# The routing's values in between in a PSUM bank, and the high-half casts of the tokens' rows on ScalarE

## The chip, the cores and the metric

The kernel runs on one core of a Trainium2 chip. The metric is the time of one execution in device microseconds. The engines are called as the profile calls them: PE (TensorE), DVE (VectorE), ACT (ScalarE), POOL (GpSimd) and SP (SyncE, which here issues DMAs).

## What is computed

Linear attention with random features for 8 batches, 8 heads, 576 tokens and a head width of 64, followed by a mixture of experts in which each token goes to one expert:

```
phi(x)  = exp(h - max(h)) / sqrt(128),  h = x @ omega.T - |x|^2 / 2        # q, k scaled by 64^-1/4
attn    = phi(q) @ (phi(k).T @ v) / (phi(q) @ sum(phi(k)) + 1e-6)          # per batch and head
x       = attn, heads side by side                                         # 4608 tokens x 512
e       = argmax(x @ w_gate);  g = softmax(x @ w_gate)[e];  s = sigmoid(x @ w_output_gate)[e]
out     = g * s * (relu(x @ w1[e]) @ w2[e])                                # 8 experts, 512 -> 1024 -> 512
```

## The kernel before

The tokens are worked through in four superchunks (j = 0 to 3) of two batches each, nine blocks of 128 tokens. For each superchunk and head there is a unit (32 in all): PE projects keys and queries (line 503, tiles pp), DVE takes the extreme value of each row (line 525) and makes the bias nb (lines 534 and 538, or 531), ACT takes the exponentials (ef, line 544), PE sums keys times values (kv, line 637), ACT or DVE splits them (kvs), PE multiplies by the queries (pn, line 681), and DVE divides (den and xf, lines 690 to 694). Nearly all products are made of fp16 pairs: a high half by a cast, and the low half as the difference, which POOL computes (lines 437, 567, 588, 715).

Two units make a pair (16 in all). Its rows xf are split into a high half (step xh, line 711, a cast on DVE with one instruction for a unit) and a low half (step xl, line 715, POOL), both in the tile xs. From there one DMA writes the rows to DRAM and another transposes them (xrt); PE makes the logits of the gates (lg, line 777), and DVE adds them up (lga).

When the four pairs of a superchunk have their logits, its routing runs, nearly all of it on DVE, in short instructions on 8 to 144 numbers a partition. The steps are called route (which expert), gates, gate_exps (ACT) and weigh (the weight of each token), counts (PE), ranks and places (each token's place within its expert). Then a listing turns it into slots of 128 tokens of one expert: table, assign, lists, pid (PE), gi, controls, and advance, which prepares the state for the next listing (the last listing has limits in its place). Up to 8, 8, 9 and then 24 slots come of the four listings. For each slot POOL gathers its rows (gx, line 1344), a DMA transposes them, PE runs the two layers of the expert (lines 1381 and 1404), ACT and DVE make the halves between them (lines 1388 and 1392), and POOL scatters the result (line 1445). Weights that change are split by ACT (line 365) and DVE (line 369). The helper `small` gives each routing value a place in SBUF under its name (r_l, r_oh, r_sm and so on), one buffer each.

The order of the work is made by a planner when the program is built. Every step has an engine, an assumed cost, the steps it comes after, a rank, and, if it needs one, a PSUM bank, which it holds until a named step frees it. There are eight banks: five of class a, three of class b (for the experts), and class e, which takes any of the eight. The planner walks through an assumed time and always takes the step that can start first, by rank among near ties. Each engine then runs its steps in that order and waits at each for what it needs.

Of the kernel before, what the change touches and what calls it, by code (L numbers as in the profile page):

```python
# [12 lines left out]
I32 = mybir.dt.int32  # L13
# [82 lines left out]
C_END = C_CHUNK + NSC * NC  # L96


def constants():
    c = np.zeros((P, C_END), np.float32)  # L100
    e = np.arange(NE)
    c[:, C_RDESC:C_LT] = np.tile(NE - e, NC)
    turn = (FIRST - e) % NE
    c[:, C_LT:C_EIDX] = (turn[None, :] < turn[:, None]).reshape(-1)
    c[:, C_EIDX:C_ITEM] = e
    c[:, C_ITEM:C_PART] = np.arange(NITEM)
    c[:, C_PART] = np.arange(P)
    c[:, C_CHUNK:C_END] = np.arange(NSC * NC) * P
# [148 lines left out]
def attention_moe(ctx: ExitStack, tc: tile.TileContext, kqt, kqn, v, om, wg, w1, w2, cf, cm, ci, out):  # L257
# [31 lines left out]
    last = const.tile([P, 1], F32, name="last")  # L289
    nc.vector.memset(last, float(FIRST) if SPECULATE else -1.0)  # L290
# [38 lines left out]
    def first_state():  # L329
        nc.vector.tensor_scalar(cnt, eidx, float(KEY * P), None, ALU.mult)  # L330
        nc.vector.tensor_scalar(done[:, 0, :], eidx, float(KEY), None, ALU.mult)
        nc.vector.tensor_copy(done[:, 1, :], eidx)
        nc.vector.tensor_copy(ahead, cft[:, C_LT : C_LT + NE * NE].rearrange("p (a b) -> p a b", a=NE))
# [120 lines left out]
    def unit(u):  # L454
# [255 lines left out]
        def hi_half():  # L710
            nc.vector.tensor_copy(halves(xs(pr).bitcast(F16)[:, :, o : o + D]), halves(xf(pr)[:, :, o : o + D]))  # L711

        def lo_half():
# [6 lines left out]
            ("xh", u), ("DVE",), 0.37, hi_half, after=[("xf", u, 0), ("xf", u, 5)], rank=R + 6,  # L720
# [87 lines left out]

    rt = {}

    def route(j):
        l2 = lga(j).rearrange("p c (a e) -> p c e a", a=2)
        l = small("l", [NC, 2 * NE])
        nc.vector.tensor_reduce(out=l, in_=l2, op=ALU.add, axis=AX.X)
        yield
        lgt, log = l[:, :, 0:NE], l[:, :, NE:]
        top = small("top", [NC])
        nc.vector.tensor_reduce(out=top, in_=lgt, op=ALU.max, axis=AX.X)
        yield

        oh = small("oh", [NC, NE])
        nc.vector.tensor_tensor(out=oh, in0=lgt, in1=bc(top), op=ALU.is_ge)
# [9 lines left out]
        nc.vector.tensor_tensor(out=one, in0=oh, in1=bc(rm), op=ALU.is_equal)  # L832
        rt[j] = dict(one=one, lgt=lgt, log=log, top=top)

    def gates(j):
        r = rt[j]
        d = small("d", [NC, NE])
        nc.vector.tensor_tensor(out=d, in0=r["lgt"], in1=bc(r["top"]), op=ALU.subtract)
        yield
        z = small("z", [NC, NE])  # L840
# [3 lines left out]
        nc.vector.tensor_reduce(out=zs, in_=z, op=ALU.add, axis=AX.X)  # L844
        r.update(d=d, zs=zs)
# [6 lines left out]
    def weigh(j):  # L852
        d, zs = rt[j]["d"], rt[j]["zs"]
        sm = small("sm", [NC])
        nc.vector.tensor_reduce(out=sm, in_=d, op=ALU.add, axis=AX.X)
        yield
        nc.vector.tensor_scalar(sm, sm, 1e-9, 1.0 / S_OUT, ALU.add, ALU.mult)
# [25 lines left out]
    def ranks(j):  # L883

        pos = banks["pos", j]
        pk = small("pk", [NC, NE])
# [8 lines left out]
        rank = small("rank", [NC])  # L895
# [3 lines left out]
    def places(j):  # L899

        rank, key = rt[j]["rank"], keys[:, j * NC : (j + 1) * NC]
        ri = small("ri", [NC], I32)
# [20 lines left out]
    def table(g):  # L923

        t = tabs[g] = {}
        av_i = small("av_i", [NE], I32)
# [4 lines left out]
        av = t["av"] = small("av", [NE])  # L931
        nc.vector.tensor_tensor(out=av, in0=av_i, in1=done[:, 0, :], op=ALU.subtract)
        yield
        t8 = small("t8", [NE, NE])
# [5 lines left out]
        start = t["start"] = small("start", [NE])  # L940
# [3 lines left out]
        off = t["off"] = small("off", [2, NE])  # L944
        nc.vector.tensor_copy(off[:, 1, :], eidx)
        yield
        nc.vector.tensor_tensor(out=off[:, 0, :], in0=done[:, 0, :], in1=start, op=ALU.subtract)
        yield
        end = t["end"] = small("end", [NE])
        nc.vector.tensor_tensor(out=end, in0=start, in1=av, op=ALU.add)  # L950

    def assign(g):
# [9 lines left out]
        ends, mine = per_slot("ends", [], K, [NE]), per_slot("mine", [], K, [NE])  # L962
# [4 lines left out]
        ex = t["ex"] = small("ex", [2, max(KS) + 1])[:, :, 0 : K + 1]  # L967
# [4 lines left out]
        both = per_slot("both", [2], K, [NE])  # L972
# [9 lines left out]
        key = t["key"] = per_slot("key", [], K)  # L982
# [3 lines left out]
    def lists(g):  # L986
# [3 lines left out]
        if g == NG - 1:  # L990
            itc = ef(FREE).rearrange("p c m -> p (c m)").bitcast(F16)[:, 0 : nt * 2 * K]
            itc = itc.rearrange("p (c a i) -> p c a i", a=2, i=K)
        else:
            itc = small("itc", [NSC * NC, 2, max(EARLIER)], F16)[:, 0:nt, :, 0:K]
# [17 lines left out]
    def controls(g):  # L1012
# [5 lines left out]
        here = per_slot("here", [], K)  # L1018
# [3 lines left out]
        nc.vector.tensor_tensor(out=sw, in0=ex[:, 1:], in1=ex[:, 0:K], op=ALU.not_equal)  # L1022
# [33 lines left out]
    def advance(g):  # L1056
# [3 lines left out]
        t1 = small("t1", [NE])  # L1060
# [7 lines left out]
        fin = per_slot("fin", [], K)  # L1068
# [4 lines left out]
        nc.vector.tensor_tensor(out=fin, in0=fin, in1=t["ex"][:, 1, 1:], op=ALU.mult)  # L1073
# [3 lines left out]
        turn = small("turn", [NE])  # L1077
        nc.vector.tensor_scalar(turn, eidx, last, float(NE), ALU.is_gt, ALU.mult)
        yield
# [5 lines left out]
            in1=turn.unsqueeze(2).broadcast_to([P, NE, NE]),  # L1085
# [26 lines left out]
    def routing(j):  # L1112
# [10 lines left out]
        chain("route", (0.37, 0.14, 0.14, 0.14, 0.14, 0.14), route, first, tiles=[("lga", j)])  # L1123
# [9 lines left out]
        chain("gates", (0.14, 0.14, 0.14), gates, [("route", j)], rank=R + 5)  # L1133
        plan.add(("gate_exps", j), ("ACT",), 0.42, lambda: gate_exps(j), after=[("gates", j)], rank=R + 5)
        chain("weigh", (0.14, 0.07, 0.07, 0.08, 0.1), weigh, [("gate_exps", j)], rank=R + 5)
# [3 lines left out]
        )  # L1139

    def listing(g):
# [10 lines left out]
        chain("table", (0.07, 0.07, 0.08, 0.13, 0.08, 0.14, 0.08, 0.08, 0.08), table, [("ranks", j), *old])  # L1152
        chain("assign", (wide, wide, 0.07, wide, 2 * wide, 2 * wide, 0.08), assign, [("table", g)])
        each = 0.06 + 0.001 * nt * K
        own = [("ef", FREE)] if g == NG - 1 else []
        chain("lists", (each, each, each), lists, [("assign", g), ("places", j)], tiles=own)
# [6 lines left out]
        if g < NG - 1:  # L1163
            chain(
                "advance", (0.07, 0.07, 0.08, 0.08, 0.08, 0.08, 0.08, 0.08, 0.08, 0.13), advance, [("controls", g)],
                rank=R + 40,
            )
        else:
            chain("limits", (0.08, wide, wide, 0.08, 0.08, 0.08, 0.08), limits, [("assign", g)], rank=R + 0.5)
# [371 lines left out]
```

## Time and profile before

| | |
|---|---|
| Three runs | 701.48 us median (699.2 to 703.88) |
| Profiled execution | 700.21 us, its span on the core 698.4 us |
| Busy in the span | PE 613.5 us, DVE 444.4, ACT 406.1, POOL 326.6 |
| Mean granted clock of PE | 0.948 |

The span runs from the first to the last instruction. An engine's busy time counts what it executes, and includes time in which an instruction has started and can't go on. In rows of groups the numbers behind the bar are busy us, mean ns of one, and the idle time of the engine just before, with what ended it. In rows of the timeline the first two numbers are start and length in us, and the brackets hold the idle time before. In rows of windows the first number behind the stretch is its length, then come the engines' busy times.

### The profile page before, as it was taken

The page shows a single profiled execution, that of the slowest core. Times are in us where ns is not written, and L with a number is a line of the kernel's source. Part 1 is how long each engine was busy: PE and PEld are TensorE (multiplying, and loading weights), DVE is VectorE, ACT ScalarE, POOL GpSimd, SP SyncE. Part 2 cuts the span into 40 slices and gives each one's busy share as a digit, 9 for nine tenths or more (in the row PEclk, how much of TensorE's full clock was granted, in tenths as well). Part 3 has the DMA queues.
Part 4 walks back from the last instruction along what each step waited for, and adds up shares of the span by engine and source line. Part 5 has one row for each costly group of instructions (what it writes and reads, how often), then busy time and mean ns, then how long its engine had stood idle before and what let it go on. Part 6 is the DMA issues. An engine that isn't in the chain of part 4 may idle for free. (4 is left out here: it accounts for less than half of the span.)

```text
span 698.4 us, 22925 instructions
## 1 busy us (share of the span) xinstructions
PE 613.5 (88%) x8763; PEld 471.3 (67%) x8763; DVE 444.4 (64%) x1260; ACT 406.1 (58%) x909; POOL 326.6 (47%) x207
## 2 busy tenths in 40 slices
PE   6999974888897987599979869999999899999982
PEld 6899863856674765577747637887777576776750
DVE  4997898966577789688648788663583521341160
ACT  5967795878686773797858538772341421431150
POOL 1333253568673875689827637964122121231210
PEclk9999996899998999799989989999999999999997
DMA  8656889999999996999999976769956634832630
GB/s 276 235 141 165 260 257 222 176 267 225 294 304 274 177 250 113 213 208 296 212 299 232 222 134 159 148 121 190 313 127 176 211 84 109 291 75 70 246 116 8
DMA packets 181033, 137.78 MB, mean 197 GB/s; under 512 B 139535, under 2 KB 162575, under 8 KB 179600
## 3 DMA queue, kind: packets, MB, share of 16 engines
q1 hardware_dynamic: 174800, 116.13, 68.2%
q0 software_dynamic: 6080, 19.72, 9.2%
q8 instruction: 83, 1.36, 0.8%
q14 instruction: 70, 0.57, 0.3%
HBM read 83.69 MB, written 19.69 MB: 148 GB/s over the span
## 5 line engine op out<-in xcount | busy, mean ns | idle before, releaser
L1381 PE MATMUL ph<-xt,w1h 128*128 128x128 f16 (+1 forms) x2432 | 205.0, 218 | 1.5 <-DMA xt<-gx 1.4
L544 ACT ACTIVATE ef<-pp,nb 128x128 f32<-128x128 f32 x576 | 164.2, 392 | 70.0 <-DVE nb L538 34.5
L1381 PE MATMUL ph<-xt,w1l 128*128 128x128 f16 (+1 forms) x1216 | 201.3, 218 | 0.4 <-DVEq L1305 0.4
L1381 PEld LDWEIGHTS <-w1h 128*128 128x128 f16 x2432 | 182.0, 99 | 8.7 <-DMA xt<-gx 1.6
L1392 DVE SCALAR_TENSOR_TENSOR hl<-ph,hh 128x512 f16<-128x512 f32 (+1 forms) x76 | 50.5, 666 | 128.9 <-ACTq L1310 77.9
L567 POOL TENSOR_TENSOR es<-ef,es 128x1152 f16<-128x1152 f32 x44 | 104.7, 2384 | 43.6 <-ACT es L565 22.6
L1404 PE MATMUL po<-w2h,hl 128*128 128x512 f16 x304 | 119.6, 393 | 5.4 <-DVE hl L1392 5.4
L1404 PE MATMUL po<-w2h,hh 128*128 128x512 f16 x304 | 120.1, 395 | 4.5 <-DVE w1l L369 2.4
L1404 PE MATMUL po<-w2l,hh 128*128 128x512 f16 x304 | 119.6, 393 | 0.0
L1381 PEld LDWEIGHTS <-w1l 128*128 128x128 f16 x1216 | 118.8, 99 | 0.6 <-DVEq L1305 0.6
L525 DVE TENSOR_REDUCE pp<-pp 128x3 f32<-128x384 f32 x192 | 102.7, 558 | 22.1 <-PE pp L503 21.7
L1344 POOL DMA_INDIRECT gx<-rows,gi x38 | 40.5, 1067 | 162.9 <-ACT os L1456 119.8
L1404 PEld LDWEIGHTS <-hh 128*128 128x128 f16 x608 | 57.3, 100 | 70.0 <-issue 9.9
L1388 ACT ACTIVATE hh<-ph 128x512 f16<-128x512 f32 (+1 forms) x76 | 44.7, 589 | 75.0 <-PE ph L1381 66.4
L1456 ACT ACTIVATE os<-po,gx 128x512 f32<-128x512 f32 x38 | 26.1, 687 | 92.5 <-PE po L1404 80.3
L715 POOL TENSOR_TENSOR xs<-xf,xs 128x576 f16<-128x576 f32 x32 | 41.1, 1285 | 64.5 <-DVE xs L711 27.5
L437 POOL TENSOR_TENSOR xlo<-xt,xhi 128x1152 f16<-128x1152 f32 x24 | 57.2, 2381 | 20.0 <-ACT xhi L430 20.0
L1404 PEld LDWEIGHTS <-hl 128*128 128x128 f16 x304 | 30.8, 101 | 45.0 <-DVE hl L1392 6.4
L503 PE MATMUL pp<-omh,xhi 64*128 64x128 f16 x432 | 45.3, 225 | 17.4 <-ACT ef L544 5.5
L565 ACT CAST es<-ef 128x1152 f16<-128x1152 f32 x44 | 51.6, 1176 | 10.7 <-DMA et<-es 8.0
L503 PEld LDWEIGHTS <-xhi 64*128 64x128 f16 x864 | 35.0, 98 | 29.1 <-issue 9.4
L681 PE MATMUL pn<-kvs,et 128*128 128x65 f16 (+1 forms) x960 | 41.2, 199 | 10.2 <-DVE kvs L659 4.1
(159 smaller groups left out, 1015.0 us busy)
## 6 DMA issues: line engine op xcount, KB each, us to landing
r<-w SPq DMA_DIRECT2D x10, 2048.0 KB, 9.4
xt<-kqt SPq DMA_DIRECT2D x32, 576.0 KB, 5.5
xn<-kqn SPq DMA_DIRECT2D x24, 576.0 KB, 7.3
rawv<-v SPq DMA_DIRECT2D x32, 325.0 KB, 5.3
rows<-xs SPq DMA_DIRECT2D x16, 576.0 KB, 5.8
r<-w SPq DMA_DIRECT2D x8, 512.0 KB, 10.3
ef<-w SPq DMA_DIRECT2D x2, 512.0 KB
et<-w SPq DMA_DIRECT2D x2, 512.0 KB, 7.6
```

Of the source, the lines that this page charges most:

```text
L437: lambda t0=t0, t1=t1: nc.gpsimd.tensor_tensor(out=xl(u)[:, t0:t1], in0=xt32(u)[:, t0:t1], in1=xh(u)[:, t0:t1], op=ALU.subtract),
L503: nc.tensor.matmul(banks["pp", 2 * u + i, g][:, c, :], x[r, t], w[r, :], start=(a == 0), stop=(a == len(ops) - 1))
L525: nc.vector.tensor_reduce(out=pp[:, 3, 0:3], in_=pp[:, 0:3, :], op=ALU.min, axis=AX.X)
L544: nc.scalar.activation(ef(n)[:, c, :], banks["pp", n, g][:, c % 3, :], AF.Exp, bias=nb(n)[:, c : c + 1], scale=-SK)
L565: nc.scalar.copy(es(slot_es(n))[:, 0], ef(n))
L567: nc.gpsimd.tensor_tensor(out=es(slot_es(n))[:, 1], in0=ef(n), in1=es(slot_es(n))[:, 0], op=ALU.subtract)
L681: nc.tensor.matmul(pn[lo:hi, c - c0, :], a[:, c, lo:hi], w[:, b, :], start=(i == 0), stop=(i == len(ops) - 1))
L715: nc.gpsimd.tensor_tensor(out=x[:, :, P + o : P + o + D], in0=xf(pr)[:, :, o : o + D], in1=x[:, :, o : o + D], op=ALU.subtract)
L1381: nc.tensor.matmul(ph[:, f4, 0:w_], w[qd][:, kk, fo : fo + P], xt(n)[:, x, 0:w_], start=(a == 0), stop=(a == 3 * KC - 1))
L1388: nc.scalar.activation(hh(n)[:, sl, 0:w_], banks["ph", n, g][:, :, 0:w_], AF.Relu)
L1392: nc.vector.scalar_tensor_tensor(out=hl(n)[:, sl, 0:w_], in0=banks["ph", n, g][:, :, 0:w_], scalar=0.0, in1=hh(n)[:, sl, 0:w_], op0=ALU.ma ...
L1404: nc.tensor.matmul(po, x(n)[:, f, :], w[f // 2][:, f % 2, :], start=(f == 0 and a == 0), stop=(f == FC - 1 and a == 2))
```

## The change

The values that a routing and its listing need only for themselves move from SBUF into one PSUM bank of 512 numbers a partition, called rt. The bank is taken at the first step of route and freed at the end of advance (in the last listing, limits). A table gives each name its place in the bank; names that aren't alive together share one. Values stay in SBUF that ACT, PE or a DMA reads, that outlive the listing, that are fp16, or that meet a PSUM value as the second operand; for some of these a copy is made (avs, exs, turns). For the last listing most values of the slots stay in SBUF. Fifty-six DVE instructions of each of the first three routings and listings then read or write the bank, and 32 of the last.

Beside that, the expert numbers in off are written once at the start and not by each listing; the sum with 1 in weigh is joined with the product behind it; the first three listings build their list matrix from one comparison and one wider product with cp, a copy of constants in the bank; the ranks of gates and of advance put these steps earlier; table waits for gates, and advance for lists, weigh and places. The planner's assumed costs follow.

The casts xh run on ACT with an assumed cost of 0.6 in place of 0.37 on DVE.

```diff
-            nc.vector.tensor_copy(halves(xs(pr).bitcast(F16)[:, :, o : o + D]), halves(xf(pr)[:, :, o : o + D]))
+            nc.scalar.copy(halves(xs(pr).bitcast(F16)[:, :, o : o + D]), halves(xf(pr)[:, :, o : o + D]))
...
-            ("xh", u), ("DVE",), 0.37, hi_half, after=[("xf", u, 0), ("xf", u, 5)], rank=R + 6,
+            ("xh", u), ("ACT",), 0.6, hi_half, after=[("xf", u, 0), ("xf", u, 5)], rank=R + 6,
...
+    def inner(j, nm, sh, dt=F32):
+
+        a, n = HOMES[nm]
...
+        t = banks["rt", j][:, a : a + size]
...
-        l = small("l", [NC, 2 * NE])
+        l = inner(j, "l", [NC, 2 * NE])
...
-        oh = small("oh", [NC, NE])
+        oh = inner(j, "oh", [NC, NE])
...
-        sm = small("sm", [NC])
+        sm = inner(j, "sm", [NC])
...
-        nc.vector.tensor_scalar(zs, zs, 1.0, None, ALU.add)
-        yield
-        nc.vector.tensor_tensor(out=sm, in0=sm, in1=zs, op=ALU.mult)
+        nc.vector.scalar_tensor_tensor(out=sm, in0=zs, scalar=1.0, in1=sm, op0=ALU.add, op1=ALU.mult)
...
+        t["av"] = small("avs", [NE])
+        nc.vector.tensor_tensor(out=t["av"], in0=av_i, in1=done[:, 0, :], op=ALU.subtract)
...
-        start = t["start"] = small("start", [NE])
+        start = t["start"] = inner(j, "start", [NE])
...
-        off = t["off"] = small("off", [2, NE])
-        nc.vector.tensor_copy(off[:, 1, :], eidx)
...
+            cp = inner(GROUPS[g], "cp", [nt, 2])
+            nc.vector.tensor_copy(cp, cft[:, C_BOTH : C_BOTH + 2 * nt].rearrange("p (c a) -> p c a", a=2))
...
-        turn = small("turn", [NE])
+        turn = inner(GROUPS[g], "turn", [NE])
         nc.vector.tensor_scalar(turn, eidx, last, float(NE), ALU.is_gt, ALU.mult)
+        yield
+        turns = small("turns", [NE])
+        nc.vector.tensor_tensor(out=turns, in0=turn, in1=eidx, op=ALU.subtract)
...
-        chain("route", (0.37, 0.14, 0.14, 0.14, 0.14, 0.14), route, first, tiles=[("lga", j)])
+        chain(
+            "route", (0.37, 0.14, 0.14, 0.14, 0.14, 0.14), route, first, tiles=[("lga", j)],
+            bank=("e", ("rt", j), [512]),
+        )
...
-        chain("gates", (0.14, 0.14, 0.14), gates, [("route", j)], rank=R + 5)
+        chain("gates", (0.14, 0.14, 0.14), gates, [("route", j)], rank=R + 0.1)
...
-                rank=R + 40,
+                [("controls", g), ("lists", g), ("weigh", j), ("places", j)], rank=R + ADV, frees=[("rt", j)],
```

Every engine's order is planned anew, and differs in many places. Three of them follow. In the rows a name with a number is a tile and its buffer, and the line numbers are those of the kernel that the row is of.

DVE in the second routing, at the table of experts and the weights of the tokens, before (line 857 is the scaling of the sums r_sm):

```order
L938 TENSOR_REDUCE r_tot<-r_av 128x1
L857 TENSOR_SCALAR r_sm<-r_sm 128x9
L941 TENSOR_REDUCE r_start<-r_t_5322 128x8
L859 TENSOR_SCALAR r_zs<-r_zs 128x9
L945 COPY r_off<-cft 128x8
L861 TENSOR_TENSOR r_sm<-r_sm,r_zs 128x9
L947 TENSOR_TENSOR r_off<-done,r_start 128x8
L863 RECIPROCAL scales<-r_sm 128x9
L950 TENSOR_TENSOR r_end<-r_start,r_av 128x8
L657 TENSOR_SCALAR kvs_5441<-kv_5325 128x130
```

The same place on DVE now, where rt_5103 is the bank:

```order
L975 TENSOR_REDUCE r_tot<-rt_5103 128x1
L892 TENSOR_SCALAR rt_5103<-rt_5103 128x9
L978 TENSOR_REDUCE rt_5103<-rt_5103 128x8
L894 SCALAR_TENSOR_TENSOR rt_5103<-r_zs,rt_5103 128x9
L982 TENSOR_TENSOR off<-done,rt_5103 128x8
L896 RECIPROCAL scales<-rt_5103 128x9
L985 TENSOR_TENSOR rt_5103<-rt_5103,r_avs 128x8
L531 TENSOR_REDUCE pp_0_5203<-pp_0_5203 128x3
```

Two instructions are gone, the others stand in the same order with an operand in the bank, and a reduction of the attention follows in place of the split kvs, which moved ahead of this piece.

DVE at the end of the second advance, before:

```order
L1075 TENSOR_REDUCE last<-r_fin 128x1
L538 SCALAR_TENSOR_TENSOR nb_5749<-pp_0_5201,sqs_3982 128x3
L1078 TENSOR_SCALAR r_turn<-cft,last 128x8
L525 TENSOR_REDUCE pp_1_5232<-pp_1_5232 128x3
L1080 TENSOR_TENSOR r_turn<-r_turn,cft 128x8
L534 SCALAR_TENSOR_TENSOR pp_1_5232<-pp_1_5232,sqs_3982 128x3
L1082 TENSOR_TENSOR ahead<-r_turn 128x64
```

The same place on DVE now:

```order
L1131 TENSOR_REDUCE last<-rt_5103 128x1
L531 TENSOR_REDUCE pp_0_5204<-pp_0_5204 128x3
L1134 TENSOR_SCALAR rt_5103<-cft,last 128x8
L531 TENSOR_REDUCE pp_1_5267<-pp_1_5267 128x3
L1137 TENSOR_TENSOR r_turns<-rt_5103,cft 128x8
L540 SCALAR_TENSOR_TENSOR pp_0_5204<-pp_0_5204,sqs_4645 128x3
L1139 TENSOR_TENSOR rt_5103<-rt_5103,cft 128x8
L544 SCALAR_TENSOR_TENSOR nb_5724<-pp_0_5204,sqs_4645 128x3
L1141 TENSOR_TENSOR ahead<-rt_5103,r_turns 128x64
```

There is one instruction more (r_turns), and the comparison that makes ahead, with which the bank is freed, has one operand in the bank and one in SBUF.

The cast of the ninth pair's first unit, which before stands on DVE within the second routing:

```order
L694 TENSOR_TENSOR xf_5182<-pn_5_5114,den_5181 128x4x64
L829 TENSOR_REDUCE r_rm<-r_oh 128x9
L711 CAST xs_5222<-xf_5182 128x2x9x32
L832 TENSOR_TENSOR r_one<-r_oh,r_rm 128x72
L838 TENSOR_TENSOR r_d<-r_l,r_top 128x72
```

and the same cast on ACT now:

```order
L550 ACTIVATE ef_5024<-pp_1_4825,nb_4814 128x128 x3
L550 ACTIVATE ef_5024<-pp_2_4847,nb_4814 128x128 x3
L449 ACTIVATE sqt_5132<-xn_4641 128x1152
L717 CAST xs_5185<-xf_5101 128x2x9x32
L571 CAST es_5223<-ef_4817 128x1152
```

The cast left DVE's queue and stands in ACT's, behind exponentials and squares of later units and ahead of the cast es.

More of the change, by code (lines that the diff above doesn't have):

```diff
@@ L807, in bc, with inner_slot @@
         return a.unsqueeze(2).broadcast_to([P, NC, NE])
+    KM = max(EARLIER)
+    HOMES = {}
+    for names, width in (
+        ("l both", 2 * KM * NE), ("oh pk mine", NC * NE), ("z t8 cp", NC * NE), ("sm fin", KM), ("rank", NC), ("av_i", NE),
+        ("av", NE), ("start", NE), ("end", NE), ("ex", 2 * KM + 2), ("key", KM), ("ri here", KM), ("t1", NE), ("turn", NE),
+    ):
+        at = max((a + n for a, n in HOMES.values()), default=0)
+        HOMES.update({nm: (at, width) for nm in names.split()})
+    assert max(a + n for a, n in HOMES.values()) <= 512 and KM >= NC and 2 * (NG - 1) <= NE
+    def inner(j, nm, sh, dt=F32):
+        a, n = HOMES[nm]
+        size = math.prod(sh)
+        assert size <= n
+        t = banks["rt", j][:, a : a + size]
+        if dt != F32:
+            t = t.bitcast(dt)
+        if len(sh) > 1:
+            names = "abc"[: len(sh)]
+            t = t.rearrange(f"p ({' '.join(names)}) -> p {' '.join(names)}", **dict(zip(names, sh)))
+        return t
+    def inner_slot(g, nm, lead, K, tail=()):
+        return per_slot(nm, lead, K, tail) if g == NG - 1 else inner(GROUPS[g], nm, [*lead, K, *tail])
     rt = {}
@@ L1139, in routing @@
         )
+    ADV = 3
     def listing(g):
```

88 lines of the change are left out of this document (59 added, 29 removed).

## Prediction

> **What bounds the kernel now.** I read the page first, for who is busy and when, then the windows, then single stretches of the timeline.
>
> ```profile
> span 698.4 us, 22925 instructions
> PE 613.5 (88%) x8763; PEld 471.3 (67%) x8763; DVE 444.4 (64%) x1260; ACT 406.1 (58%) x909; POOL 326.6 (47%) x207
> PE   6999974888897987599979869999999899999982
> DVE  4997898966577789688648788663583521341160
> PEclk9999996899998999799989989999999999999997
> ```
>
> PE is the long engine. The digits show where it is not: around slices 6, 16 and 23 it drops, DVE stands at 8 or 9 there, and the granted clock dips behind. The next view sums these places, the stretches from a routing's first instruction to the last of its list, and the halves of the program.
>
> ```profile
> core 0: us, PE busy (x) PEld busy (x) DVE busy (x) ACT busy (x) POOL busy (x), PEclk, DMA share, GB/s
> 99.00:126.00 27.00, 14.73 (x225) 12.74 (x224) 24.65 (x98) 15.63 (x45) 13.45 (x8) 0.70 0.86 212
> 251.00:284.00 33.00, 23.80 (x343) 17.14 (x340) 30.79 (x97) 13.94 (x31) 17.93 (x11) 0.95 0.81 168
> 389.00:416.00 27.00, 19.95 (x339) 15.50 (x336) 25.90 (x79) 9.29 (x19) 13.43 (x8) 0.89 0.87 180
> 0.00:480.00 480.00, 413.43 (x6373) 328.59 (x6374) 366.82 (x1112) 340.51 (x817) 284.08 (x168) 0.94 0.90 218
> 480.00:686.00 206.00, 200.05 (x2391) 142.75 (x2389) 77.58 (x149) 65.57 (x92) 41.55 (x38) 0.99 0.56 161
> ```
>
> Up to 480 us PE idles 66.6 us; behind that, 6.0 of 206. So what PE gains before 480 moves the end, and nothing after it can. In the three routing stretches PE idles 12.3, 9.2 and 7.1 us, 28.5 together, while DVE is busy 81.3 of 87: there DVE is the bound. The fourth routing, behind 480, is covered by PE's queue of experts and is counted at nothing.
>
> DVE is not working all that time. These rows are of the timeline, DVE's instructions with POOL's beside two of them, and PE behind each.
>
> ```profile
> 252.41 2.36 DVE L822 TENSOR_TENSOR r_oh<-r_l,r_top 128x72 f32<-128x72 f32 x1
> 256.06 0.19 PE L871 MATMUL pos<-r_one,cmt 128*128 128x72 f16 x1 [1.54 <-DVE r_one L832]
> 261.82 4.46 DVE L857 TENSOR_SCALAR r_sm<-r_sm 128x9 f32<-128x9 f32 x1
> 263.84 2.40 POOL L567 TENSOR_TENSOR es<-ef,es 128x1152 f16<-128x1152 f32 x1
> 267.55 0.84 PE L681 MATMUL pn<-kvs,et 128*128 128x65 f16 x12 [4.08 <-DVE kvs L659]
> 275.58 4.27 DVE L1078 TENSOR_SCALAR r_turn<-cft,last 128x8 f32<-128x8 f32 x1
> 277.45 2.37 POOL L437 TENSOR_TENSOR xlo<-xt,xhi 128x1152 f16<-128x1152 f32 x1
> 281.69 0.21 PE L503 MATMUL pp<-omh,xhi 64*128 64x128 f16 x1 [2.14 <-ACT ef L544]
> ```
>
> An instruction on nine numbers takes 4.46 us and ends at 266.28; POOL's subtraction ends at 266.24. The third ends at 279.85, POOL at 279.82. So a small DVE instruction whose operands are all in SBUF stands until POOL's instruction is through, and PE idles behind it.
>
> **The change, part by part.** First, the waits. The groups of equal instructions give the undisturbed size and who never waits:
>
> ```profile
> L857 DVE TENSOR_SCALAR r_sm<-r_sm 128x9 f32<-128x9 f32 x4 | 5.0, 1246 | 0.0
> L534 DVE SCALAR_TENSOR_TENSOR pp<-pp,sqs 128x3 f32<-128x3 f32 x144 | 22.3, 163 | 1.0 <-DVEq L1305 0.3
> L887 DVE TENSOR_TENSOR r_pk<-pos,cnt 128x72 f32<-128x72 f32 x4 | 0.9, 224 | 0.5 <-PE pn L681 0.5
> L844 DVE TENSOR_REDUCE r_zs<-r_z 128x9 f32<-128x72 f32 x4 | 0.9, 224 | 0.0
> L950 DVE TENSOR_TENSOR r_end<-r_start,r_av 128x8 f32<-128x8 f32 x4 | 0.6, 144 | 0.0
> ```
>
> L534 has one operand in PSUM and one in SBUF; 144 of them average 163 ns, so POOL doesn't hold them up. The change gives nearly every routing instruction of the first three routings this form. I count only waits with a PE gap behind. The second stretch: 1.54 + 4.08 + 2.14 = 7.8 us, each gap shorter than the wait ahead of it (2.1, 4.3 and 4.1, if the short forms take 0.2). First and third stretch:
>
> ```profile
> 112.22 2.20 DVE L947 TENSOR_TENSOR r_off<-done,r_start 128x8 f32<-128x8 f32 x1
> 115.52 0.28 PE L503 MATMUL pp<-omh,xhi 64*128 64x128 f16 x1 [2.91 <-DVE r_ex L968]
> 399.81 2.42 DVE L907 CAST keys<-r_ri 128x9 f32<-128x9 int32 x1
> 404.78 1.10 PE L637 MATMUL kv<-vs,es 128*128 128x65 f16 x30 [1.61 <-DVE xf L694]
> 411.33 2.53 DVE L996 TENSOR_TENSOR r_itc<-keys,r_key 128x243 f16<-128x243 f32 x1
> 414.72 0.87 PE L1093 MATMUL pid<-r_itc,place 128*128 128x18 f16 x27 [3.93 <-DVE ctl L1024]
> ```
>
> L947 should take 0.16, so 2.0 of the 2.91 go. Of the third stretch go the 1.6, and of the 3.93 the 2.1 by which L996 is longer than the 0.4 that I estimate for its 243 numbers between L844 (72 numbers, 224 ns) and L525 (384 numbers, 4.36 / 8 = 0.55 us, in a row below). Sum **-13.5**. Its ends: 0, if every gap is filled by another wait, and -28.5, all idle of the three stretches.
>
> Second, PE's clock.
>
> ```profile
> 109.80:126.80 17.00, 8.01 (x98) 7.12 (x98) 14.65 (x59) 7.58 (x21) 8.90 (x6) 0.50 0.75 182
> sum 40.80, PE 26.10 PEld 20.79 DVE 33.87 ACT 21.11 POOL 20.98; mean PE 5.22 PEld 4.16 DVE 6.77 ACT 4.22 POOL 4.20
> ```
>
> Five stretches at 0.50 in or behind the routings (at 109.8, 266.8, 283.9, 389.7 and 413.6) hold 26.1 us of PE work, 13 us of it due to the clock. With half of the gaps gone some of them won't be granted down; most of what they slow lies beside a busy DVE. Between 0 and -13 I take **-3**.
>
> Third, the casts of the high halves (xh). They leave DVE and go to ACT.
>
> ```profile
> 255.42 0.45 DVE L711 CAST xs<-xf 128x576 f16<-128x576 f32 x1
> L711 DVE CAST xs<-xf 128x576 f16<-128x576 f32 x32 | 23.4, 731 | 0.2
> L583 ACT CAST vs<-rawv 128x650 f16<-128x650 f32 x20 | 15.3, 767 | 0.9 <-PE kv L637 0.6 <-ACTq L1305 0.2
> L544 ACT ACTIVATE ef<-pp,nb 128x128 f32<-128x128 f32 x576 | 164.2, 392 | 70.0 <-DVE nb L538 34.5 <-DVE nb L531 12.0 <-issue 6.4
> ```
>
> DVE loses 23.4 us (the undisturbed cast takes 0.45, the mean holds the same waits for POOL). Outside the routings DVE seldom has PE waiting, so of 0 to -23.4 I take **-1**. On ACT, between 392 ns for 128 elements and 767 for 650, one of 576 costs 0.71, times 32 is 22.7 us. The cover is ACT's idle time: 139.5 us before 480, 46.5 of it ahead of the exponentials, waiting for DVE's biases (nb). Behind a cast in ACT's queue stand exponentials, which free the banks of the projections (pp). If three of the 32 casts stand before an exponential that PE waits for, that is **+2**; with no cover, +22.7.
>
> Fourth, the bank. Each routing now holds one of eight PSUM banks from its first sum to the last use in advance (last group: limits).
>
> ```profile
> 99.00:126.00 27.00, 4.36 (x8) 0.70 0.86 212
> 251.00:284.00 33.00, 3.34 (x6) 0.95 0.81 168
> 389.00:416.00 27.00, 2.68 (x5) 0.89 0.87 180
> PE pp L503 <- ACT ef L544: 5.9, 8, 2.1
> ```
>
> The first rows count L525's reductions in the three stretches, 8 + 6 + 5 = 19, two for a projection step: ten steps. A wait for a bank costs PE 5.9 / 8 = 0.74 us, 2.1 at most. Four of ten steps waiting once more is **+3**; ends 0 and +21. It is paid beside a DVE that is late anyway, hence nearer the low end.
>
> Fifth, added instructions (avs, exs, turns, cp) less those gone (off's copy, the +1 of zs): one more of about 0.16 us for each routing, and a wider product for itc: **+0.5**, ends 0 and +2.
>
> Whether an operand in PSUM makes an instruction longer: L887 reads PSUM, L844 SBUF, both on 72 numbers a row, both 224 ns. On a few numbers L534 takes 163, L950 with all in SBUF 144. I take 0; the upper end is 19 ns for the 56 instructions of each of three routings that touch the bank, +3.
>
> The sum: -13.5 - 3 - 1 + 2 + 3 + 0.5 = -12. The profiled execution took 700.2 us around its span of 698.4, 1.3 under the median of 701.5. **700.2 - 12 = 688.**
>
> **The rivals.**
> - *The bank becomes the wait.* With one bank less, all ten steps wait 2.1 us, +21 in place of +3, and the gaps keep the clock down (no -3): 688 + 18 + 3 = **709**, slower. Without the bank the sum is -15, so it decides from 1.5 us for a step and is slower by 1% from 2.2. For it: PE already waits for banks in these stretches (2.14 behind ACT, 2.91 behind DVE). Against: those waits end when DVE catches up, and DVE gets faster.
> - *Another wait takes the gaps.* Of the 13.5 only the two gaps that a stalled row feeds directly (4.08 and 1.54) close, the clock gives nothing: -5.6 - 1 + 2 + 3 + 0.5 = -1, **699**, no change. For it: behind a DVE that is busy 30.79 of 33 us PE finds the next late result soon. Against: the wait is time in which DVE does nothing at all.
> - *The whole wait comes back.* In a stretch that DVE bounds, all waits count, not only those with a gap behind: -24 of the 28.5 and -5 of the clock in place of -13.5 and -3, **676**.
> - *The moved instructions get longer.* At 19 ns on 168 of them, 3.2 us in stretches that DVE bounds: **691**. For it L534 against L950, against it L887 and L844. [...]
> - *PSUM doesn't help*: with one SBUF operand left the instructions still stand behind POOL. Then +5.5 - 1 on 700, **705**. L534 with 163 ns speaks against it.
>
> **How the numbers follow.** Forecast (680 to 694) 0.49; longer instructions 0.05; whole wait 0.08; another wait 0.18; PSUM doesn't help 0.04; the bank 0.16. The first three are faster by over 1%, the next two within, the last slower. Leaving out the bank's case and the tail below leaves a range of 673 to 705; the forecast's own is 680 to 694. A measurement of this kernel tells about 1% from no change, so faster means under 694.5 and slower over 708.5: 0.62, 0.22, 0.16.
>
> **What would show it.** Right: no routing instruction of the first three routings longer than its short form; PE's gaps behind kvs and r_one gone; less time at 0.50; a cast on ACT of 0.71. Wrong: PE waits for ACT's exponentials in the three stretches for much over 6 us; ACT idle only little before 480; new long gaps at lg, whose rows go through ACT now (cast, POOL, transposing DMA). It would also be wrong if the order, planned anew on every engine, puts steps where their inputs are late.

## The result, and the profile after

The changed kernel takes **680.32 us** (median of four runs, 676.38 to 684.09) against 700.67 us of the kernel before on the same chip. The ratio is 0.970, with an interval from 0.964 to 0.977. A second measurement on another chip (below) gave 0.973, from 0.968 to 0.979. Here and below a ratio leaves out executions that ran over 1.5% above the fastest of their kernel, so it is not the quotient of the medians. The forecast was 688 in a range of 673 to 705, its own part of it 680 to 694. The profiled execution took 679.76 us around a span of 678.0, where before it was 700.21 around 698.4.

The page of the changed kernel, with each engine's busy time and the digits of 40 slices:

```profile
span 678.0 us, 22927 instructions
PE 610.9 (90%) x8763; PEld 473.6 (70%) x8763; DVE 397.9 (59%) x1232; ACT 423.2 (62%) x941; POOL 324.6 (48%) x207
PE   6999875699979999699989999999999999999982
DVE  4897667766576669566688885531782611430160
PEclk9999967599998999699999999999999999999997
```

DVE lost 46.5 us of busy time, ACT gained 17.1, and PE's is 2.6 shorter. PE's idle time, the span less its busy time, fell from 84.9 us to 67.1. So the 20.4 us of the span are 17.8 of idle time and 2.6 of shorter work. In PE's digits (counted from 1) the dip at slice 24 is gone and slice 21 is up from 7 to 8, and of the dip at 16 and 17 a single slice is left. The dip from 6 to 8 is still there.

To see where the idle time went, the same stretches are laid over both kernels: each routing from its sum of the logits to the end of advance. First the kernel before, then the changed one. Behind the stretch stand its length and PE's busy time, and DVE's is the third of the engines. The last row of the second fence, in answer to the prediction's, is the time up to 480 us.

```profile
99.00:125.30 26.30, 14.03 (x214) 12.20 (x213) 23.95 (x98) 15.02 (x42) 12.98 (x7) 0.70 0.86 210
251.20:280.70 29.50, 22.72 (x324) 16.45 (x321) 28.41 (x94) 11.42 (x23) 17.73 (x11) 0.94 0.82 168
389.40:422.80 33.40, 26.35 (x389) 18.85 (x386) 30.73 (x102) 14.13 (x34) 17.03 (x11) 0.85 0.77 168
```

```profile
98.60:122.70 24.10, 14.38 (x189) 13.06 (x190) 18.02 (x91) 12.70 (x31) 10.73 (x7) 0.71 0.55 143
247.30:270.40 23.10, 21.62 (x333) 15.36 (x331) 20.93 (x95) 15.76 (x32) 14.70 (x10) 1.00 0.91 211
376.50:399.20 22.70, 21.99 (x393) 16.84 (x389) 19.62 (x99) 16.10 (x34) 19.18 (x12) 1.00 0.99 227
0.00:480.00 480.00, 432.19 (x6668) 348.18 (x6669) 326.42 (x1098) 365.49 (x859) 288.55 (x174) 0.95 0.92 229
```

PE idled 12.3, 6.8 and 7.1 us in the three routings, 26.1 together. Now it idles 9.7, 1.5 and 0.7, which is 11.9. So 14.2 of the 17.8 us went there. In the second and third the granted clock is 1.00 and PE hardly stops. In the first it still stands for 40% of the time.

The instructions that stood for POOL are short. These are groups of equal instructions of the changed kernel: r_sm's scaling, keys and turn had means of 1246, 734 and 1571 ns. The fourth row (pk, at 224 before) had not waited. The last two are the cast on ACT and the exponentials.

```profile
L892 DVE TENSOR_SCALAR rt<-rt 128x9 f32<-128x9 f32 x4 | 0.7, 174 | 0.1
L940 DVE CAST keys<-rt 128x9 f32<-128x9 int32 x4 | 0.7, 167 | 0.1
L1134 DVE TENSOR_SCALAR rt<-cft,last 128x8 f32<-128x8 f32 x3 | 0.7, 222 | 0.2 <-DVEq L1373 0.2
L920 DVE TENSOR_TENSOR rt<-pos,cnt 128x72 f32<-128x72 f32 x4 | 0.9, 236 | 0.1
L717 ACT CAST xs<-xf 128x576 f16<-128x576 f32 x32 | 21.9, 685 | 16.5 <-DVE xf L700 12.7 <-issue 3.4
L550 ACT ACTIVATE ef<-pp,nb 128x128 f32<-128x128 f32 x576 | 162.4, 395 | 27.6 <-DVE nb L544 12.1 <-DVE nb L537 6.2 <-DVE pp L540 3.1
```

ACT's exponentials waited 46.5 us for DVE's biases before and wait 18.3 now: 28 us less, more than the 21.9 us of casts that ACT has taken over. Half of it comes with the place of the values: in the changed order with the values in SBUF (the first experiment) they waited 32.7.

### The profile page after: what moved, and what is told of

It reads as the page before. It is cut to its first block, busy times and chain, and to the rows that moved or that the text cites. A ratio compares the mean times of both kernels' runs of the same rounds, so it can differ in the third digit from the quotient of the medians.

```text
span 678.0 us, 22927 instructions
## 1 busy us (share of the span) xinstructions
PE 610.9 (90%) x8763; PEld 473.6 (70%) x8763; DVE 397.9 (59%) x1232; ACT 423.2 (62%) x941; POOL 324.6 (48%) x207
## 5 line engine op out<-in xcount | busy, mean ns | idle before, releaser
L550 ACT ACTIVATE ef<-pp,nb 128x128 f32<-128x128 f32 x576 | 162.4, 395 | 27.6 <-DVE nb L544 12.1
L1472 PE MATMUL po<-w2h,hh 128*128 128x512 f16 x304 | 115.4, 380 | 3.3 <-DVE hl L1466 2.1
L1472 PE MATMUL po<-w2l,hh 128*128 128x512 f16 x304 | 115.2, 379 | 0.9 <-DVE w2l L375 0.9
L1472 PE MATMUL po<-w2h,hl 128*128 128x512 f16 x304 | 115.2, 379 | 0.8 <-DVE hl L1460 0.8
L1472 PEld LDWEIGHTS <-hh 128*128 128x128 f16 x608 | 55.4, 98 | 65.2 <-issue 3.3
L687 PE MATMUL pn<-kvs,et 128*128 128x65 f16 (+1 forms) x960 | 41.3, 199 | 13.5 <-DMA et<-es 8.7
L687 PEld LDWEIGHTS <-et 128*128 128x128 f16 (+1 forms) x960 | 35.2, 102 | 21.6 <-DMA et<-es 10.0
```

The lines of the kernel that those rows point to most:

```text
L550: nc.scalar.activation(ef(n)[:, c, :], banks["pp", n, g][:, c % 3, :], AF.Exp, bias=nb(n)[:, c : c + 1], scale=-SK)
L687: nc.tensor.matmul(pn[lo:hi, c - c0, :], a[:, c, lo:hi], w[:, b, :], start=(i == 0), stop=(i == len(ops) - 1))
L1472: nc.tensor.matmul(po, x(n)[:, f, :], w[f // 2][:, f % 2, :], start=(f == 0 and a == 0), stop=(f == FC - 1 and a == 2))
```

## Experiments

The theory: the whole gain comes from where the values lie, since a small DVE instruction with all operands in SBUF stands while POOL works and one with an operand in PSUM doesn't. The rivals: the new order or the joined instructions bring it; the casts on ACT bring it; the bank costs part of it.

All twelve are listed here. Each ratio is against the kernel before on the same chip. That kernel's median was 697.6 us on the chip of the first four rows, 700.9 on that of the next four and 695.3 on that of the last four, so medians of different groups can't be set against each other.

| Kernel | median us | ratio, interval |
|---|---|---|
| values in SBUF, same order | 696.0 | 1.001 (0.997 to 1.006) |
| bank, casts on DVE | 670.8 | 0.959 (0.951 to 0.968) |
| the casts alone on ACT | 699.2 | 1.001 (0.997 to 1.005) |
| values in SBUF, no bank, planned anew | 704.5 | 1.015 (1.008 to 1.022) |
| casts on ACT in the order planned for DVE | 677.6 | 0.964 (0.954 to 0.974) |
| casts on DVE in the order planned for ACT | 684.1 | 0.981 (0.975 to 0.988) |
| first routing in SBUF | 682.4 | 0.978 (0.969 to 0.986) |
| second and third routing in SBUF | 699.3 | 0.999 (0.995 to 1.004) |
| whole change again | 677.1 | 0.973 (0.968 to 0.979) |
| bank, casts on DVE, again | 673.3 | 0.971 (0.967 to 0.976) |
| whole change, planned anew | 677.7 | 0.977 (0.972 to 0.982) |
| bank, casts on DVE, planned anew | 681.8 | 0.977 (0.971 to 0.983) |

### The same order, the values back in SBUF

```diff
-        t = banks["rt", j][:, a : a + size]
+        if ("rts", j) not in live:
+            live["rts", j] = sb.tile([P, 392], F32, tag="rts", name=f"rts{j}", bufs=1)
+        t = live["rts", j][:, a : a + size]
```

> The changed kernel with the routing's values in one SBUF tile of the same layout in place of the bank. The bank is still held by the planner and left unused, so every engine has the changed kernel's order. If the waits for POOL made the gain: DVE instructions of the routings again last 1 to 4.5 us and end with POOL's, 15 to 30 us more in all on DVE, and the time goes back by 8 to 16 us, to 688 to 697. If the new order, the earlier advance or the cast on ACT made it: 677 to 684, as the changed kernel.

It measured 696.0 us, in the band expected for the waits, and the ratio is 1.001: with order, instructions, held bank and casts of the change, nothing of the gain is left. The stretches of this kernel (windows, columns as above) and rows of its timeline, DVE's and POOL's, show why. Here rts is the tile in SBUF.

```profile
98.00:126.90 28.90, 15.75 (x205) 14.28 (x203) 23.38 (x90) 13.85 (x32) 11.97 (x7) 0.68 0.54 131
246.10:278.10 32.00, 26.42 (x365) 18.23 (x362) 30.66 (x95) 16.47 (x33) 18.75 (x11) 0.89 0.80 198
380.00:415.40 35.40, 25.83 (x402) 19.40 (x399) 33.05 (x99) 16.58 (x35) 21.52 (x13) 0.90 0.67 161
```

```profile
380.99 2.39 POOL L443 TENSOR_TENSOR xlo<-xt,xhi 128x1152 f16<-128x1152 f32 x1
383.31 1.29 POOL L721 TENSOR_TENSOR xs<-xf,xs 128x576 f16<-128x576 f32 x1
384.54 2.37 POOL L573 TENSOR_TENSOR es<-ef,es 128x1152 f16<-128x1152 f32 x1
380.99 6.03 DVE L859 TENSOR_TENSOR rts<-rts,r_top 128x72 f32<-128x72 f32 x1
386.94 0.55 DVE L531 TENSOR_REDUCE pp<-pp 128x3 f32<-128x384 f32 x1
```

DVE's busy time in the three stretches is 87.1 us here and 58.6 in the changed kernel, 28.5 less for the same instructions in the same order. PE idles 28.3 us here and 11.9 there, 16.4 less. So in these stretches 58% of the time in which DVE stood came back to PE.

That share is a local one. Over the whole of the two profiled executions PE's idle time is 77.0 and 67.1 us, 9.9 apart, and the spans are 690.2 and 678.0, 12.2 apart. This execution took 692.0 us, near the fast end of ten between 690.5 and 700.7. By the ratios, 1.001 against 0.970 and 0.973, the place of the values is worth 2.8 to 3.1%, some 20 to 22 us, give or take 5. The runs agree that the place brings the gain, and leave open whether half or three quarters of DVE's time came back.

One comparison on 72 numbers took 6.03 us, and ended (387.02) when three POOL instructions that followed each other were all through (386.91). The same comparison in the third routing of the changed kernel runs beside a subtraction of POOL too:

```profile
376.13 2.40 POOL L443 TENSOR_TENSOR xlo<-xt,xhi 128x1152 f16<-128x1152 f32 x1
377.43 0.24 DVE L857 TENSOR_TENSOR rt<-rt,r_top 128x72 f32<-128x72 f32 x1
```

So beside POOL the comparison took 6.03 us with both inputs in SBUF, and 0.24 with one in the bank.

But not every instruction with all operands in SBUF stands, though the prediction and the theory have it so. No reduction of the three routings stood in the kernel before: those on 72 numbers took 211 to 230 ns, one of them (r_zs, from 257.51) 0.21 us while a subtraction of POOL ran from 257.25 to 258.66. Here three on 72 numbers take 0.21 to 0.23 us, and the last section shows one of them beside POOL. Casts and scalings with a single input in SBUF did stand (before, the scaling of r_sm for 4.46 us and the cast keys for 2.42).

### Which routing brings it

Both kernels keep the order of the change; the condition in the first line is `j == 0` in one and `j in (1, 2)` in the other.

```diff
+        if j == 0:
+            if ("rts", j) not in live:
+                live["rts", j] = sb.tile([P, 392], F32, tag="rts", name=f"rts{j}", bufs=1)
+            t = live["rts", j][:, a : a + size]
+        else:
+            t = banks["rt", j][:, a : a + size]
```

> The whole change in its own order, with the values of the first routing alone in SBUF again. In the whole change PE's idle time between 80 and 140 us was as long as before (18.3 and 18.4 us), while it fell by 6 us in the second routing and by 10 in the third. Theory, in the first routing other waits (for keys transposed by DMA, for exponentials) take the gaps, so nothing is lost by going back: 678 to 683. Rival, each routing brings its third of the 16 us that all of them bring: 684 to 688.

> The complement: the values of the second and third routing in SBUF again, those of the first and fourth in the bank, order unchanged. Theory, the whole gain of the place lies in these two: 693 to 698, like the kernel with all of them in SBUF (696.0). Rival, thirds: 689 to 692.

With the first routing in SBUF the ratio is 0.978, with the second and third 0.999. The two rows are groups of the kernel with the first routing in SBUF: the same product in the first routing, and in the three others.

```profile
L977 DVE TENSOR_TENSOR rts<-ahead,rts 128x64 f32<-128x64 f32 x1 | 2.4, 2386 | 0.0
L977 DVE TENSOR_TENSOR rt<-ahead,rt 128x64 f32<-128x64 f32 x3 | 0.7, 225 | 0.1
```

So the second and third routings hold all of the gain that can be told from none: without them 0.999 is left, and the theory's side of that pair held. What the first holds is not settled. The 682.4 us lie in the band of its theory, but the two measurements of the whole change (0.970 and 0.973) stand 0.5 to 0.8% below 0.978, with intervals that overlap; that is 3 to 5 us, and the rival said 4 to 8.

Why it is little can be seen. These rows of the changed kernel are PE's in the first routing and, the last one, just behind it, with three of DVE and ACT from the longest gap. The brackets hold the idle time ahead of each.

```profile
109.86 0.17 DVE L985 TENSOR_TENSOR rt<-rt,r_avs 128x8 f32<-128x8 f32 x1
110.21 0.15 DVE L544 SCALAR_TENSOR_TENSOR nb<-pp,sqs 128x3 f32<-128x3 f32 x1
110.45 1.89 ACT L550 ACTIVATE ef<-pp,nb 128x128 f32<-128x128 f32 x6 [2.76 <-DVE nb L544]
111.39 4.59 PE L643 MATMUL kv<-rawv,ef 128*128 128x130 f32 x20 [5.09 <-ACT ef L550]
119.83 0.28 PE L509 MATMUL pp<-omh,xhi 64*128 64x128 f16 x1 [1.52 <-DVEq L1373]
121.27 0.29 PE L509 MATMUL pp<-omh,xhi 64*128 64x128 f16 x1 [1.15 <-DVE xf L700]
130.92 1.93 PE L687 MATMUL pn<-kvs,et 128*128 128x65 f16 x30 [2.47 <-DMA et<-es]
```

The longest gap ends with ACT's exponentials, and ACT had itself waited 2.76 us for a bias (nb). On DVE that bias stands behind instructions of the routing alone, from 105.07 to 110.03, every one in its short form. So here PE waits for the work of the routing and not for POOL, and the place of the values can't take this gap away: it is 5.55 us with the first routing in SBUF. The next gap ends with a branch in DVE's queue (line 1373, whether an expert's weights change), and the one behind the routing with the queries' exponentials (et; the expectation above calls them keys) transposed by DMA.

### The casts

The casts alone on ACT, as the only edit to the kernel before, and the casts back on DVE, as the only edit to the change:

```diff
-            nc.vector.tensor_copy(halves(xs(pr).bitcast(F16)[:, :, o : o + D]), halves(xf(pr)[:, :, o : o + D]))
+            nc.scalar.copy(halves(xs(pr).bitcast(F16)[:, :, o : o + D]), halves(xf(pr)[:, :, o : o + D]))
...
-            ("xh", u), ("DVE",), 0.37, hi_half, after=[("xf", u, 0), ("xf", u, 5)], rank=R + 6,
+            ("xh", u), ("ACT",), 0.6, hi_half, after=[("xf", u, 0), ("xf", u, 5)], rank=R + 6,
```

> The kernel before with only the cast xh moved to ACT (assumed cost 0.6, order planned anew). By the prediction's terms (-1 on DVE, +2 on ACT) 698 to 704, the routing's waits still there. If the cast's move was most of the gain: 680 to 690.

The second kernel has these lines the other way round.

> The changed kernel with the cast xh back on DVE (assumed cost 0.37, order planned anew). If the waits of the routing are most of it: the casts wait for POOL again, 5 to 10 us on DVE, little of it at PE: 680 to 688. If the cast's move was most of the gain: 692 to 700.

Alone, the casts on ACT change nothing that can be seen (1.001, to half a per cent). With the bank, the kernel with its casts on DVE measured 670.8 us, below what was expected, and by the ratios 1% under the whole change. One reading is that ACT is the dearer engine for them. Crossing order and engine puts that to the test: the steps stand where they were planned for one engine and the casts run on the other. The first pair of lines is against the kernel planned for DVE, the second against the whole change.

```diff
 # order planned for ("DVE",), 0.37; the cast itself on ACT
-            nc.vector.tensor_copy(halves(xs(pr).bitcast(F16)[:, :, o : o + D]), halves(xf(pr)[:, :, o : o + D]))
+            nc.scalar.copy(halves(xs(pr).bitcast(F16)[:, :, o : o + D]), halves(xf(pr)[:, :, o : o + D]))
 # order planned for ("ACT",), 0.6; the cast itself on DVE
-            nc.scalar.copy(halves(xs(pr).bitcast(F16)[:, :, o : o + D]), halves(xf(pr)[:, :, o : o + D]))
+            nc.vector.tensor_copy(halves(xs(pr).bitcast(F16)[:, :, o : o + D]), halves(xf(pr)[:, :, o : o + D]))
```

> The kernel with the bank and the casts of the high halves on DVE took 670.8 us, the whole change 680.3. They differ in the engine of the 32 casts and in the order that was planned around them. Here the order is the one that was planned for the casts on DVE, and the casts alone run on ACT, at the same places of the program. Theory 1, ACT is the dearer engine for them (685 ns each in a queue of exponentials, for which PE waits in the first 140 us): about 680, 677 to 688. Rival, the order made the difference: 668 to 674.

> The other half of the cross: the order of the whole change, the casts back on DVE at the same places. Theory 1, ACT is the dearer engine: 668 to 675. Rival, the order made the difference: 678 to 683. If both crosses lie between, each has a part; if both are slower than their planned twins, an order suits only the engine it was planned for.

The reading was not borne out. In the order of the whole change, casts on DVE measured 684.1 us, above both bands, where ACT should have been the dear one. In the other order the 677.6 us with casts on ACT lie in the band of the reading, but that band was set by times of another chip, and the ratio is 0.964 against DVE's 0.959, with intervals that overlap. The last four runs put the two kernels on one chip, and beside each the same kernel planned with another assumed cost of the cast:

```diff
-            ("xh", u), ("ACT",), 0.6, hi_half, after=[("xf", u, 0), ("xf", u, 5)], rank=R + 6,
+            ("xh", u), ("ACT",), 0.69, hi_half, after=[("xf", u, 0), ("xf", u, 5)], rank=R + 6,
...
-            ("xh", u), ("DVE",), 0.37, hi_half, after=[("xf", u, 0), ("xf", u, 5)], rank=R + 6,
+            ("xh", u), ("DVE",), 0.45, hi_half, after=[("xf", u, 0), ("xf", u, 5)], rank=R + 6,
```

> The whole change once more, so that it stands beside the next three kernels on one chip. If its first measurement holds, 0.970 of the time before, 677 to 683.

> The bank with the casts of the high halves on DVE and the order planned for that, once more beside the whole change. Theory, it is really faster than the whole change: 668 to 674, its ratio's interval clear of the other's. Rival, the one per cent between their ratios (0.959 and 0.970) was chance: 675 to 681.

> The whole change, with one number other: the planner's assumed cost of the cast on ACT is 0.69, near the measured 685 ns, in place of 0.6. No instruction is other than in the whole change, only the order that follows from the plan. Theory, an order planned anew is worth about one per cent either way, whatever it was planned for: anything from 671 to 690. Rival, the order as such is worth nothing and 0.970 is the place of the values and the engine: 677 to 683.

> The bank with the casts on DVE, planned with 0.45 for the cast, its undisturbed length in the trace, in place of 0.37. Theory that casts on DVE are better in themselves: 667 to 675 again. Rival, the 670.8 was a lucky order: 676 to 688, as with the order of the whole change (684.1).

The two kernels are 0.973 and 0.971 now, with intervals that overlap almost wholly, so the 1% between them was not borne out. Planned anew they are both 0.977. For the casts on DVE that is 0.6% over the first order on the same chip, with intervals that overlap, and 1.8% over its first measurement (0.959), which was on another chip. So the engine of the casts can't be told from the order. What an order is worth is not settled either: the four ratios of the last chip lie within 0.6%, and all their intervals overlap.

The casts' groups in the kernel with bank and casts on DVE, in its second measurement and planned anew, show what the casts pay on DVE:

```profile
L717 DVE CAST xs<-xf 128x576 f16<-128x576 f32 x32 | 25.8, 806 | 0.2
```

```profile
L717 DVE CAST xs<-xf 128x576 f16<-128x576 f32 x32 | 32.7, 1023 | 0.4
```

A cast from SBUF to SBUF takes 0.45 us undisturbed (the shortest of 32 in the kernel before 449 ns); on DVE the mean is 0.81 and 1.02, since some of these casts wait for POOL as the routing's values did: in the second kernel one takes 2.47 us from 147.49, and ends at 149.96, when POOL's subtraction has ended at 149.65, and in the kernel before one takes 3.06 us from 314.66, and ends at 317.72, POOL's subtraction at 317.38. Why they wait more in one order than in the other stays open.

### The bank

```diff
-            bank=("e", ("rt", j), [512]),
...
-                [("controls", g), ("lists", g), ("weigh", j), ("places", j)], rank=R + ADV, frees=[("rt", j)],
+                [("controls", g), ("lists", g), ("weigh", j), ("places", j)], rank=R + ADV,
```

This goes on top of the first experiment (values in SBUF), with limits edited in the same way, so the planner has all eight banks again and plans anew.

> As the run with the values in SBUF and the changed kernel's order, but no bank is held in the planner, so the order is planned anew with eight banks. The price of the bank by the prediction is +3: 685 to 694, 0 to 6 us under that run. If the bank costs much (rival: +18): 10 us or more under it.

It is 1.3% slower than with the bank held, 704.5 against 696.0 on the same chip, and over what was expected. No row shows a free bank costing time, so the likelier cause is the new order; that is argued and not shown. What the bank costs by itself can't be separated from the order by such an edit. What is shown is that the kernel that holds it is not the slower one.

## Why the prediction came out as it did

**The waits.** Forecast -13.5 of PE's idle time in the routings, measured -14.2 between the kernels before and after, and -16.4 in one and the same order. The -14.2 holds whatever the bank cost in these stretches, for which the sum had +3. The mechanism and its place were right: the gap of 4.08 us behind kvs and that of 1.54 behind r_one are gone. The first sign, no routing instruction longer than its short form, holds but for one value that stayed in SBUF, the cast that makes gi:

```profile
266.33 0.85 DVE L1164 CAST gi<-r_gid 128x8 uint32<-128x8 f32 x1
```

By routing the forecast was 2.0, 7.8 and 3.7; measured were 2.6, 5.3 and 6.3 over stretches that reach to the end of advance. So the total was met better than its parts. The 2.6 of the first is no gain yet: from 80 to 140 us PE idles 18.4 us before and 18.3 now.

**The clock.** Forecast -3; PE's busy time fell by 2.6. All stretches at half clock before its last work are summed here for before, then for after (PE's sum is the second number):

```profile
sum 64.70, PE 48.13 PEld 31.48 DVE 49.07 ACT 36.43 POOL 27.24; mean PE 4.81 PEld 3.15 DVE 4.91 ACT 3.64 POOL 2.72
```

```profile
88.40:102.05 13.65, 11.56 (x64) 10.55 (x65) 9.09 (x36) 9.15 (x27) 3.65 (x3) 0.50 0.66 217
276.20:286.40 10.20, 7.73 (x120) 7.08 (x121) 8.14 (x29) 9.50 (x25) 7.82 (x6) 0.50 0.91 248
sum 51.15, PE 38.42 PEld 35.18 DVE 37.64 ACT 36.35 POOL 23.07; mean PE 7.68 PEld 7.04 DVE 7.53 ACT 7.27 POOL 4.61
```

The work at half clock fell from 48.1 us to 38.4. How much of these 9.7 us is due to the clock is an estimate: in the kernel before, 15 products ph take 1.57 us from 283.90 to 294.10, at 0.50, and 241 take 14.27 us from 300 to 345, at 1.00, so 105 ns against 59, and by that ratio 4.2 of the 9.7 us. The busy time as a whole fell by 2.6; the forecast lies between. The size is not firm: in the profiled execution of the second measurement of this kernel PE's busy time is 607.3 us, 6.2 under the kernel before. The time at half clock didn't only shrink: the three stretches between 340 and 425 us are gone, and one from 88 us is new. The kernel with the casts alone on ACT has that one too (its start is at 88.3), and so have kernels with the casts on DVE (87.7 in the order planned for ACT), while the whole change planned anew has not. So it goes with the order and not with the engine of the casts. That gaps bring the clock down was the author's estimate; no run shows what does.

**The casts, -1 and +2.** The duration on ACT was right, 685 ns for the 0.71 forecast. The net of +1 can't be told from nothing: 1.001 alone, and 0.973 against 0.971 with the bank, each to half a per cent, which is 3 us. ACT has 114.5 us of idle time before 480 left.

**The bank, +3.** No price was seen. PE's waits for the exponentials that free the projections' banks were 5.9 us in 8 waits before, and no kernel planned with the bank waits longer (1.6 to 5.6). The first row is of the changed kernel, the next of the same order with the values in SBUF, the third of the change planned anew:

```profile
PE pp L509 <- ACT ef L550: 2.4, 5, 1.1
```

```profile
PE pp L509 <- ACT ef L550: 2.8, 4, 1.7
```

```profile
PE pp L509 <- ACT ef L550: 5.4, 6, 1.5
```

So the fall to 2.4 can't be put down to a faster DVE: with DVE standing for POOL in the same order it is 2.8, a second profile of the changed kernel has 3.6, and the other plan of the same instructions has 5.4 at about the same time (0.977). That the waits went down can be luck of the order, and what a held bank costs in one and the same order no run shows.

A sign of a wrong forecast was long gaps at lg, whose rows now go through ACT, POOL and the transposing DMA. Gaps at lg that end with this DMA (xrt) were 9.0 us in 5 before, 5.0 the longest. The profile after has none, the second measurement of the same kernel these, which are no new ones:

```profile
PE lg L783 <- DMA xrt<-xs: 3.1, 2, 2.4
```

**Added instructions and length.** The +0.5 was not measured by itself. For the length I took 0 of 0 to 19 ns. The undisturbed groups of pk, which read a PSUM value before too and whose result has moved, give 236 against 224. In the same order, the scaling of sm gives 174 in the bank and the cast keys, which reads the bank and writes SBUF, 167; with the values in SBUF they are

```profile
L894 DVE TENSOR_SCALAR rts<-rts 128x9 f32<-128x9 f32 x4 | 0.7, 168 | 0.0
L942 DVE CAST keys<-rts 128x9 f32<-128x9 int32 x4 | 0.7, 172 | 0.0
```

That is -5 to 12 ns, or at most 2 us for 168 instructions.

**The sum.** 688 was 8 us over the 679.8 of the profiled execution, which lies at the edge of the forecast's own 680 to 694. The costs for bank and ACT, +5, were not seen, and idle time outside the three routings fell by 3.6 us, for which the sum had nothing. That last part is a difference of two orders. The one pair in which two plans of the same instructions stand clear of each other on one chip, the values in SBUF with and without the bank, is 1.3% apart, so 3.6 us can be the order alone. That waits and clock together came so near (-16.5 forecast, -16.8 in the two profiles) is in part luck, as the parts of both show.

**The rivals.** The bank as the wait is out (no loss, and no longer waits). "PSUM doesn't help" is out by 6.03 against 0.24. "Another wait takes the gaps" holds in part of the first routing alone, where PE still idles 9.7 us. "The whole wait comes back" is too much by the stretches, 16.4 of 28.5 us; but its time, 676, is nearer to the measured 680 than 688 is. By the ratios the place is worth 20 to 22 us, give or take 5, between the 16.5 that the forecast has for waits and clock and the 29 of this rival.

## What to carry to other kernels

Where the trace shows a DVE instruction on a few numbers that takes microseconds and ends with an instruction of POOL, look at where its operands lie: one operand in PSUM made the same instruction in the same order short (0.24 us in place of 6.03), and 392 numbers of one bank were enough for a whole routing. Count of the time freed what PE idles behind those waits: beside the waits a little over half of DVE's standing time came back (16.4 of 28.5 us). Reductions had nothing to gain, for none of the routings' stood in the kernel before (211 to 230 ns on 72 numbers). Where a planner lays the order out, measure an edit in the unchanged order and in a second plan before putting a per cent down to it; the waits in one profile, too, can be those of its order.

## What the runs showed of the hardware

One DVE instruction on eight numbers, with its operands in SBUF, stood through two POOL instructions that followed each other, for 5.25 us. In the kernel with the same order and the values in SBUF:

```profile
272.31 2.38 POOL L443 TENSOR_TENSOR xlo<-xt,xhi 128x1152 f16<-128x1152 f32 x1
274.63 2.38 POOL L573 TENSOR_TENSOR es<-ef,es 128x1152 f16<-128x1152 f32 x1
271.79 5.25 DVE L1136 TENSOR_SCALAR rts<-cft,last 128x8 f32<-128x8 f32 x1
```

DVE's scaling of eight numbers is shown from 271.79, beside a gather of POOL that ends at 272.29, and ends at 277.04, when the second subtraction is through (277.01).

Another stood through one of two alone, for 2.34 us. In the same trace:

```profile
252.53 2.38 POOL L573 TENSOR_TENSOR es<-ef,es 128x1152 f16<-128x1152 f32 x1
254.87 1.42 POOL L594 TENSOR_TENSOR vs<-rawv,vs 128x650 f16<-128x650 f32 x1
252.66 2.34 DVE L928 TENSOR_TENSOR rts<-rts,r_one 128x72 f32<-128x72 f32 x1
255.12 0.21 DVE L931 TENSOR_REDUCE rts<-rts 128x9 f32<-128x72 f32 x1
255.46 0.86 DVE L938 CAST rts<-rts 128x9 int32<-128x9 f32 x1
```

The product L928 ends at 255.00, when the first subtraction is through (254.91), while the next runs on to 256.29. The reduction behind it takes its short 0.21 us beside that second one, and the cast after it stands to the end (256.32). What decides who comes next is not shown.

POOL's instructions took longer beside some of DVE's as well. In the third routing of this kernel its subtraction from 392.30 takes 3.42 us where the others on as many numbers take 2.38, beside DVE's product place on 1152 numbers, with both inputs in SBUF, from 392.11 to 393.47. In the changed kernel its subtraction vs from 344.44 takes 2.40 us, where the median of 20 is 1.42, beside DVE's splits of weights (w1l, line 375), four in 7.90 us from 342.30 where their median is 1.22 each.
